# Batch 0's head rearranged: separate PSUM places, no dummy matmuls, other orders on every engine

## The chip, the cores and the metric

The kernel runs on one core of a Trainium2 chip. The metric is the device time of one execution in microseconds (us). Each version is run several times and its median is given; a profiled execution of each version shows what every engine did and when. The engines are TensorE (PE; its weight loads are shown as PEld), VectorE (DVE), ScalarE (ACT), GpSimd (POOL) and SyncE (SP). Each works through its own instruction queue in order, and semaphores tie the queues together. Loads and stores are DMAs, issued from the queues of SP, ACT and POOL.

## The reference

Inputs are q, k and v with 8 batches, 8 heads, 576 positions and 64 columns a head, and the weights of a channel mix: two vectors mu of 512, w_k (512 x 1024), w_v (1024 x 512) and w_r (512 x 512). All are float32.

```
# efficient attention, per batch and head
q_s = exp(q - max) ;  q_s = q_s / sum over d
k_s = exp(k - max) ;  k_s = k_s / sum over s
x   = q_s @ (k_s.T @ v)                 # heads side by side: 8 x 576 x 512
# channel mix, per batch
x_prev = x shifted by one position (first one zero)
xk = mu_k * x + (1 - mu_k) * x_prev ;  xr = mu_r * x + (1 - mu_r) * x_prev
k  = relu(xk @ w_k) ;  v = (k * k) @ w_v ;  r = sigmoid(xr @ w_r)
out = r * v                              # 8 x 576 x 512
```

## The kernel before

**Tiling.** A batch's attention is done in two groups (g = 0, 1) of four heads; a tag such as `01` is batch 0, group 1. A group has two halves (a further digit, 0 or 1), which batches 0 and 1 load and treat one by one. 128 positions-by-head rows lie on the partitions, 9 positions of 64 columns behind each other (`J` = 9). The channel mix works on column units of a ring of four batches (`UNITS`): 11 units in all, each with eight k pieces (`k1_3` is unit 1, piece 3), each followed by `relu` on ScalarE and `sq` (the square) on VectorE. Then come 36 output tiles of 128 positions: `r12` and `v12_0`, `v12_1` are matmuls, `th12` a tanh on ScalarE (the sigmoid), `o12` the gating on VectorE, `st12` the store.

**The steps of batch 0, per group.** `load..` DMAs bring q, k and v. `expq` and `expk` (ScalarE) take exponentials. `rsum` (VectorE) sums each row of q over d, `rrec` takes the reciprocal, `scale` multiplies. `T` (TensorE) turns q, `Z` sums k's exponentials over the positions and `KV` multiplies them with v. `rz` and `kvn` (VectorE) divide the product by those sums. `qt..0` and `qt..1` copy the two halves of the turned q from PSUM, `edge` copies the column that the shift by one needs. `wp` (VectorE or GpSimd) multiplies the small k-v matrix with mu and with 1 - mu: `wp000` for xk (last digit 0) and `wp001` for xr (1). `X` (TensorE) multiplies these with the turned q and its shifted copy, so that attention and the shift's mix are one product: `X0101` is group 01, m = 0 (xk), position half 1. There are eight X groups of eight matmuls in batch 0. Copies in lower case (`x0101a`, `x0010`) take them to the tensors xk and xr, from which the k and r matmuls start. Batch 1 goes the same way (`FUSED`), later batches another way with blocks `TKV` and `B`.

**The mus.** `rows` and `muload` bring the two mu vectors by DMA. `wide` (L273) is a float32 matmul that spreads them over all partitions; `widecopy` (L291) takes it from PSUM, `rest` (L287) computes 1 - mu beside it, and `mucopy` (L296) copies a small turned form. `wp` needs `rest`.

**Dummy matmuls.** `fill` (L303, 19 matmuls of 512 columns) and `fillgap` (L312, 11 of 256 columns) multiply a zeroed tile into PSUM places that nobody reads.

**Orders.** Nothing is scheduled by a compiler. The string `ORDER` lists every step once; each engine gets its steps in that order. A word such as `ACT!qt011:0` gives the engine, the step and the index of the buffer or PSUM place that it takes (`load00v^expq000` waits for expq000 beside its own inputs). GpSimd's queue holds the loads of all batches from 1 on and the weight loads, as well as `wp`s and casts of v.

**PSUM.** There are four single places `mm` and two double places `att`. `any` 0 and 1 are the two `att`, `any` 2 and 3 are pairs of `mm` (`SHARED`). In batch 0 a group's turned q, its sums and its k-v product share one place:

```
qtp = kvp = Slot("any")
```

so that group's place is free only when the q copies and `kvn` have read it.

Of the kernel before, what the change touches and what calls it, by code (L numbers as in the profile page):

```python
# [8 lines left out]
ACT = mybir.ActivationFunctionType  # L9
# [21 lines left out]
         "mm": 4, "att": 2, "any": 4}  # L31
SHARED = {("any", 0): [("att", 0)], ("any", 1): [("att", 1)],
          ("any", 2): [("mm", 0), ("mm", 1)], ("any", 3): [("mm", 2), ("mm", 3)]}
# [13 lines left out]
ident SP!load00q0:0 ACT!load00q1 zero ACT!load01q1:1 SP!load01q0 fill:0 fill.2:1 fill.3:2 fill.4:3  # L47
fill.5:0 fill.6:1 fill.7:2 fill.8:3 fill.9:0 fill.10:1 fill.11:2 fill.12:3 fill.13:0 fill.14:1
# [10 lines left out]
load11k0 k1_0:1 relu1_3:1 sq1_7 k0_5 expq110:2 k0_0:3 load11v0 k1_0.2 k0_0.2 relu0_4:2 rsum110:2  # L59
k1_4:0 relu1_0:0 k1_5:2 sq1_3 expq111 k1_2:1 sq0_4 k1_5.2 sq1_0 k1_2.2 rsum111 relu1_5:1 k1_4.2  # L60
cast111:0 k0_1 relu1_2:2 k0_6:2 sq1_5 wv0 relu1_4:0 k1_6:1 rrec110 expq101:1 sq1_2 k0_2:0
scale110:2 load10k1:9 k0_6.2 relu0_0:1 X0111:1 load10v0 rrec111 k0_7 expq100 rsum101:3 k1_6.2
k1_1:3 relu0_6:2 load10k0 k0_2.2 rrec101 k1_1.2 sq0_0 ACT!x0111 k0_3 rsum100 wv1 r0:2 relu1_1:1
sq0_6 expk111:2 wv2 r1:3 sq1_4 rrec100 th0:0 load20q0:10 scale100:0 relu1_6:2 r2:2 th1:1
load21q0:0 sq1_6 scale111 ACT!cast110 r3:1 sq1_1 relu0_2:0 scale101 T11:0 expk110 T10:1
ACT!cast101:1 KV11 qt101:2 load20v0:1 v3_0:3 qt110:1 sq0_2 th3:2 qt111 v0_0:0 rz11:2 expk101:0
cast100 kvn11:0 DVE!qt100 v1_0:1 edge11 expk100 wp110:0 edge10 DVE!wp111 X1100:0 KV10 x1100 v0_1
rz10:0 kvn10:1 X1111:0 POOL!wp100:1 X1101:1 x1111 v1_1 ACT!x1101 load31q0:2 X1001:0 th2:3 X1000:1
load20k0:3 ACT!x1001 v0_2 DVE!x1000 v3_1 load21v0:4 expq200:0 o0 v1_2 load21k0:5 k2_7:2 k2_3:0
rsum200:1 expq210:2 wp101 k2_7.2 v3_2 load30q0:6 relu2_7:2 o1 X1011:0 X1110:1 cast200:2 load30k0:7  # L70
rrec200 k2_3.2 o3 k2_1:2 load40q0:8 k2_0:1 relu2_3:1 x1011 k2_1.2 load30v0:9 expq310:1 sq2_3
k2_0.2 scale200:1 load41q0:10 k2_2:3 k2_6:0 relu2_1:0 load31k0:0 relu2_0:1 X1010:0 k2_2.2
expk200:1 sq2_0 k2_6.2 DVE!x1010 k2_5:2 load31v0:1 v2_0:1 relu2_2:1 sq2_1 rsum210:0 cast210:0
k2_4:3 load40k0:2 TKV20:0 relu2_6:0 sq2_2 rrec210 expk210:2 k2_4.2 rz20:1 sq2_6 k2_5.2 sq2_7
load40v0:3 v6_0:0 DVE!x1110 relu2_5:1 relu2_4:0 w20:0 v2_1 scale210:2 expq300:0 r5:2 load50q0:4
r6:3 qt20:0 rsum310:2 load50k0:5 v2_2 expk300:0 sq2_5 B21:1.0 sq2_4 o2 load41v0:6 th6:4 v6_1
rz21:2 xb20:0 w21:1 rsum300:3 r4:1 load50v0:7 xs20 qt21:1 r7:3 edge20 o6 th4:5 rrec300 X21:0.1
st6.2 diff20:0 th7:6 r8:0 th5:7 sc2001:0 scale300:0 v4_0:1 xb21:1 v5_0:3 xs21 sc2011:1 cast300:1
sc2010 v7_0:2 sc2000 edge21 rrec310 expq400:2 diff21:1 load70k0:9 TKV30:0 sc2100:2 expq410:0 v5_1
sc2101 load70v0:8 rz30:0 mix210 v4_1 cast310:2 load51v0:10 mix200 v7_1 o5 th8:8 v4_2 load51q0:1  # L80
sc2111:2 k3_1:3 st5.2 expk400:1 o4 w30:2 k3_3:0 st4 o7 relu3_1:2 load41k0:2 st0.2 expk310:2 sc2110
k3_7:1 mix201 st1 k3_0:3 sq3_1 st6 qt30:2 load51k0:0 scale310:1 st5 k3_2:2 relu3_0:1 st1.2
cast400:0 sq3_0 B31:1.0 rsum400:1 relu3_2:0 k3_6:3 load60k0:3 xs30:0 mix211 relu3_7:2 k3_5:2
relu3_3:1 rz31:1 sq3_2 xb30 w31:0 k3_4:1 sq3_3 sq3_7 relu3_6:0 r9:0 edge30 rrec400 diff30:0 qt31:0
r12:3 sq3_6 scale400:2 relu3_5:1 B40:0.1 th9:9 v10_0:2 relu3_4:2 sc3001:0 sq3_5 xs31:1 xb31 sq3_4
r10:0 sc3000 sc3011:1 expk500:0 v10_1 edge31 rsum410:0 v8_0:1 th10:4 load61k0:5 diff31:1 expq500:1
v11_0:0 o10 v8_1 expq510:2 load60v0:4 mix300 r11:2 sc3100:2 th12:7 sc3101 load70q0:1 mix310
cast510:1 v9_0:3 rsum500:3 v11_1 th11:1 load60q0:10 k4_5:2 o8 rz40:2 rrec410 k4_6:1 sc3111:0
relu4_5:0 rrec500 o11 k4_2:2 sc3110 st11.2 sc3010 k5_0:0 scale500:0 st2.2 relu4_2:1 v9_1 st7.2
relu4_6:2 cast410:2 st2 k4_3:2 sq4_2 sq4_5 o9 tq40^load60q0:1 k5_4:1 relu4_3:1 k5_1 scale410:1  # L90
expq600:1 k4_0:3 sq4_6 k5_5 tq41^load60q0:2 relu4_0:0 rsum510:2 k5_6:2 relu5_4:2 k4_1:3 expk410:2
tq50^load60q0:0 w40:1 k4_4:1 sq4_0 sq5_4 relu5_0:0 mix301 k5_7 st11 cast500:0 B41:1.0 mix311 st4.2
relu5_6:2 k4_7:0 st7 rz41:0 sq5_0 rrec510 st0 relu4_1:0 sq4_3 r13:2 rsum600:1 st8 xs40:0 relu4_4:1
# [806 lines left out]
```

## Time and profile before

| what | value |
|---|---|
| median of 3 runs | 196.46 us (196.37 to 196.91) |
| profiled execution | 196.49 us |
| its span, first to last instruction | 194.7 us |
| TensorE busy | 184.9 us (95%) |
| VectorE busy | 148.4 us (76%) |
| ScalarE busy | 133.7 us (69%) |
| GpSimd busy | 46.4 us (24%) |
| DMA | 42.45 MB, 218 GB/s mean |

Rows of the timeline give the start in us from the span's start, the length in us, the engine, the line of the kernel, the operation, the tiles written and read with their shapes, and how many instructions the row holds; a bracket at the end gives the engine's idle time before it and what ended it. In the list of waits, each row gives who waited, for what, the total in us, how often, and the longest. Rows of the chain of waits give start, length and what held up the end of the run. Rows by stretch give, after the stretch and its length, the busy time of TensorE, its weight loads, VectorE, ScalarE and GpSimd (with instruction counts), TensorE's granted clock, the share of the DMA engines that was busy, and GB/s. Matmuls overlap in their pipeline, so the distance between two starts, not a matmul's own length, is its cost in a dense stretch.

### The profile page before, as it was taken

How to read it: one execution, taken by the hardware profiler on the slowest of the kernel's cores; microseconds unless marked ns; L12 is line 12 of the kernel's file. 1: busy time of each engine (PE TensorE's matmuls, PEld its weight loads, DVE VectorE, ACT ScalarE, POOL GpSimd, SP SyncE). 2: the span in 40 equal slices, each digit the busy share in tenths (PEclk: the TensorE clock that was granted, in tenths of full speed). 3: DMA queues.
4: the chain of work that ended last, by engine and by line, in shares of the span. 5: the costliest groups of instructions: out<-in, count | busy, mean ns of one | idle time of the engine just before them, and what ended most of it. 6: DMA issues, size and time to landing. Idle time of an engine off the chain costs nothing.

```text
span 194.7 us, 4639 instructions
## 1 busy us (share of the span) xinstructions
PE 184.9 (95%) x1819; PEld 93.9 (48%) x1841; DVE 148.4 (76%) x343; ACT 133.7 (69%) x214; POOL 46.4 (24%) x76
## 2 busy tenths in 40 slices
PE   7897999999999999999999999999999999999990
PEld 2374755445545544465545644444444444444450
DVE  1886887689999999998998998999669247324431
ACT  3856999899999999489997988663175522621400
POOL 6857663885416303200700000000000000000000
PEclk9999999999999999999999999999999999999998
DMA  5999999999999999979997794144015003703855
GB/s 190 350 204 338 300 306 307 327 397 394 391 392 394 400 411 331 331 246 203 231 407 183 179 206 88 32 100 96 7 35 130 0 0 83 188 3 80 201 123 135
DMA packets 26069, 42.45 MB, mean 218 GB/s; under 512 B 11828, under 2 KB 15168, under 8 KB 26048
## 3 DMA queue, kind: packets, MB, share of 16 engines
q0 software_dynamic: 9504, 28.00, 43.8%
q1 hardware_dynamic: 15728, 12.72, 27.1%
q10 hardware_dynamic: 816, 1.44, 2.0%
q8 instruction: 14, 0.23, 0.5%
q14 instruction: 7, 0.06, 0.1%
HBM read 33.56 MB, written 9.44 MB: 221 GB/s over the span
## 4 chain that ended last, share of the span: by engine, by line
PE 80%; DVE 7%; DMA 6%; issue 2%; ACT 1%; POOL 1%; ACTq 0%; DVEq 0%; POOLq 0%
PE mm_c L681 10%; PE mm_b L734 9%; PE mm_a L734 8%; PE mm_d L734 8%; PE mm_b L681 8%; PE mm_d L681 7%; PE mm_c L714 5%; PE mm_c L734 4%; PE mm_a L681 4%; PE mm_d L714 4%; PE mm_a L714 3%; DMA mu_rows<-in_moe_mu_r_dram 3%; DMA raw_c<-in_q_dram 3%; PE mm_b L714 3%; DVE k L670 1%
## 5 line engine op out<-in xcount | busy, mean ns | idle before, releaser
L734 PEld LDWEIGHTS <-k 128*128 128x128 bf16 x296 | 28.1, 98 | 30.6 <-issue 0.7
L714 PEld LDWEIGHTS <-xr 128*128 128x128 bf16 x144 | 13.9, 98 | 16.4 <-issue 0.2
L670 DVE TENSOR_TENSOR k<-rel_b 128x512 bf16<-128x512 bf16 (+2 forms) x29 | 11.6, 399 | 8.9 <-ACT rel_b L660 8.8
L660 ACT ACTIVATE rel_a<-mm_c 128x512 bf16<-128x512 f32 (+1 forms) x11 | 6.6, 599 | 9.7 <-PE mm_c L681 9.6
L714 PE MATMUL mm_c<-wr,xr 128*128 128x512 bf16 x47 | 12.3, 379 | 0.1
L681 PEld LDWEIGHTS <-wk_aa 128*128 128x128 bf16 x88 | 8.4, 98 | 7.8 <-issue 0.2
L681 PEld LDWEIGHTS <-wk_ba 128*128 128x128 bf16 x88 | 8.3, 98 | 7.8 <-issue 0.4
L670 DVE TENSOR_TENSOR k<-rel_a 128x512 bf16<-128x512 bf16 (+2 forms) x24 | 9.6, 400 | 3.2 <-ACT rel_a L660 3.2
L670 DVE TENSOR_TENSOR k<-rel_c 128x512 bf16<-128x512 bf16 (+2 forms) x23 | 9.3, 403 | 3.4 <-ACT rel_c L660 3.3
L681 PEld LDWEIGHTS <-wk_ab 128*128 128x128 bf16 x88 | 8.4, 98 | 7.1 <-issue 0.5
L681 PEld LDWEIGHTS <-wk_bb 128*128 128x128 bf16 x88 | 8.5, 98 | 6.8
L734 PE MATMUL mm_b<-wv_a,k 128*128 128x512 bf16 x42 | 11.2, 379 | 0.1
L714 PE MATMUL mm_d<-wr,xr 128*128 128x512 bf16 x40 | 10.3, 379 | 0.0
L734 PE MATMUL mm_a<-wv_a,k 128*128 128x512 bf16 x38 | 10.2, 379 | 0.1
L734 PE MATMUL mm_d<-wv_a,k 128*128 128x512 bf16 (+1 forms) x38 | 9.8, 368 | 0.1
L681 PE MATMUL mm_c<-xk,wk_ba 128*128 128x512 bf16 (+3 forms) x34 | 8.6, 334 | 0.0
L681 PE MATMUL mm_c<-xk,wk_bb 128*128 128x512 bf16 (+3 forms) x34 | 8.6, 334 | 0.0
L714 PE MATMUL mm_a<-wr,xr 128*128 128x512 bf16 x31 | 8.2, 380 | 0.1
L660 ACT ACTIVATE rel_c<-mm_c 128x512 bf16<-128x512 f32 (+1 forms) x8 | 4.8, 595 | 4.5 <-PE mm_c L681 2.9
L681 PE MATMUL mm_c<-xk,wk_aa 128*128 128x512 bf16 (+2 forms) x28 | 7.4, 347 | 0.0
L681 PE MATMUL mm_c<-xk,wk_ab 128*128 128x512 bf16 (+2 forms) x26 | 7.0, 344 | 0.0
L660 ACT ACTIVATE rel_b<-mm_d 128x512 bf16<-128x512 f32 (+2 forms) x10 | 5.8, 577 | 1.5 <-PE mm_d L681 1.5
(352 smaller groups left out, 495.4 us busy)
## 6 DMA issues: line engine op xcount, KB each, us to landing
raw_k<-in_q_dram POOLq DMA_DIRECT2D x4, 576.0 KB, 8.1
raw_f<-in_k_dram POOLq DMA_DIRECT2D x3, 576.0 KB, 8.2
raw_a<-in_k_dram POOLq DMA_DIRECT2D x3, 576.0 KB, 11.5
out_dram<-th_b SPq DMA_DIRECT2D x10, 128.0 KB, 2.4
out_dram<-th_c SPq DMA_DIRECT2D x10, 128.0 KB, 2.4
raw_b<-in_v_dram POOLq DMA_DIRECT2D x2, 576.0 KB, 10.4
raw_d<-in_k_dram POOLq DMA_DIRECT2D x2, 576.0 KB, 8.8
raw_e<-in_v_dram POOLq DMA_DIRECT2D x2, 576.0 KB, 6.3
```

What stands on the lines that cost most here:

```text
L660: kn.nc.scalar.activation(out=kn.rels[rel.index][:, 0:width], in_=kn.bank(kf)[:, 0:width], func=ACT.Relu, scale=HALF_ROOT)
L670: kn.nc.vector.tensor_tensor(out=to, in0=src, in1=src, op=ALU.mult)
L681: kn.nc.tensor.matmul(kn.bank(kf)[:, lo:lo + n], lhsT=kn.wk[fc // 4][ct % 2][:, ct // 2, (fc % 4) * 128: (fc % 4) * 128 + 128], rhs=kn.xs[ ...
L714: kn.nc.tensor.matmul(kn.bank(rps), lhsT=kn.xs[1][:, ct, c:c + 128], rhs=kn.wr[:, ct, :], start=(ct == 0), stop=(ct == CT - 1))
L734: kn.nc.tensor.matmul(kn.bank(vps)[:, 0:width], lhsT=kn.k2[:, ft, at:at + 128], rhs=wv_of(ft)[:, part], start=(ft == 0), stop=(ft == FT - 1))
```

## The change

It has five parts.

- In batch 0 the turned q goes to a place of a new kind, `pr` (two pairs of `mm`), and the sums and the k-v product to an `att` place. `KV` now follows `Z` in the same place.
- `rest` (1 - mu) and `mucopy` go from VectorE to ScalarE.
- In batches 0 and 1 reciprocal and scaling of q are done once a group, not once a half. In group 00 and in batch 1 the row sums stay in halves; in group 01 they too become one instruction (`rsum010`).
- The 30 dummy matmuls are left out (`FILLS`, `GAPS`). `WHOLE_Q` is defined and not used.
- `ORDER` is another one from the first step to the last. It also changes the engine of some steps: in batch 1 all four casts of v go to GpSimd (two of them were on ScalarE), in batch 0 `wp010` goes to GpSimd and `wp001` to VectorE (the other way round before), and all eight X groups of batch 0 stand ahead of the first k step (seven before, with `X0111` later).

```
 POOLS = {...
-         "mm": 4, "att": 2, "any": 4}
+         "mm": 4, "att": 2, "any": 4, "pr": 2}
 SHARED = {("any", 0): [("att", 0)], ("any", 1): [("att", 1)],
...
+          ("pr", 0): [("mm", 0), ("mm", 1)], ("pr", 1): [("mm", 2), ("mm", 3)]}
-FILLS = 19
-GAPS = 11
+FILLS = 0
+GAPS = 0
+WHOLE_Q = True
 ORDER = """
-ident SP!load00q0:0 ACT!load00q1 zero ACT!load01q1:1 SP!load01q0 fill:0 fill.2:1 fill.3:2 fill.4:3
...
-fill.15:2 fill.16:3 fill.17:0 fill.18:1 fill.19:2 POOL!rows consts ACT!load00k1:2 SP!load00k0 late
-ACT!load01k1:3 SP!load01k0 warm POOL!muload expq000:0 expq001 load00v^expq000 rsum000:0 rsum001
-load01v expq010:1 wk00 expq011 rrec001 rrec000 rsum010:1 wide:0 wk01 expk000:0 rrec010 rsum011
-wk10 mu:1 expk001 fillgap:2 fillgap.2:3 fillgap.3:2 fillgap.4:3 scale010:0 wk11 Z00:0 fillgap.5:2
-fillgap.6:3 fillgap.7:2 fillgap.8:3 fillgap.9:2 fillgap.10:3 fillgap.11:2 rrec011 expk011:1
-load11q0:4 scale011 widecopy rz00:0 scale001:1 T01:1 KV000 scale000 ACT!qt011:0 KV001 expk010
-DVE!qt010 T00 rest mucopy kvn00:0 KV010 qt001:1 POOL!wp001:0 DVE!qt000 Z01 KV011 edge00 load10q0:5
-wp000 X0010:3 rz01:1 load11q1 X0001:2 kvn01:1 edge01 x0010 wp010:1 load10q1 X0000:0 wp011 x0001a
-X0100:1 load11v1:6 ACT!x0001b X0110:3 x0000a wr X0101:2 x0100b ACT!x0000b x0110 X0011:0 load11k1:7
-DVE!x0101a x0100a k0_4:2 x0101b k1_7:3 x0011 k1_3:0 load10v1:8 k1_7.2 k1_3.2 relu1_7:0 k0_4.2
...
+ident SP!load00q0:0 ACT!load00q1 zero ACT!load01q1:1 SP!load01q0 POOL!rows consts ACT!load00k1:2
+SP!load00k0 late ACT!load01k1:3 SP!load01k0 warm POOL!muload expq000:0 expq001 load00v^expq000
+rsum000:0 rsum001 load01v expq011:1 wk00 expq010 rrec000 scale000:0 wide:0 wk01 expk001:0 wk10
+mu:1 expk000 rsum010:1 T00:1 wk11 Z00:0 expk010:1 load11q0:4 rrec010 rz00:0 scale010:1 widecopy
+load10q1:5 mucopy KV000 load11q1 expk011 KV001 DVE!qt000:0 ACT!qt001 Z01:1 rest kvn00:0 T01:0
+edge00 rz01:1 KV010 wp001:0 ACT!qt011:1 KV011 wp000 X0011:3 kvn01:1 X0000:0 DVE!qt010 POOL!wp010:1
+ACT!x0011 X0010:1 x0000b X0001:2 wr DVE!x0000a x0010 X0101:3 edge01 wp011 ACT!x0001b X0100:0
+load11k0:6 x0001a DVE!x0101a X0110:1 load10q0 ACT!x0101b DVE!x0100a X0111:2 load11k1 k1_3:2
+ACT!x0100b k1_2:3 ACT!x0111 k1_3.2 k1_2.2 relu1_3:0 k1_7:0 load11v1:7 k0_4:1 relu1_2:1 k1_4:2
...
     def emit_rest():
-        kn.nc.vector.tensor_scalar(out=kn.mu_wide[:, 1, :], in0=kn.mu_wide[:, 0, :],
-                                   scalar1=-1.0, scalar2=1.0, op0=ALU.mult, op1=ALU.add)
+        kn.nc.scalar.activation(out=kn.mu_wide[:, 1, :], in_=kn.mu_wide[:, 0, :], func=ACT.Copy,
+                                scale=-1.0, bias=1.0)
...
-    wide_done = add("DVE", emit_rest, [wide_a], name="rest")
+    wide_done = add("ACT", emit_rest, [wide_a], name="rest")
...
+        expq = [add("ACT", lambda u=u: exp(kn.eqs, eq, sq, u), [lq[n], table], [eq], [sq],
+                    name=f"expq{tag}{n}") for n, u in enumerate(us)]
+        if b < 2:
+            parts = us if b or g == 0 else [slice(0, 2)]
+            o = [add("DVE", lambda u=u: rsum(u), expq[u], [stat], name=f"rsum{tag}{n}")
+                 for n, u in enumerate(parts)]
+            o = add("DVE", lambda: rrec(slice(0, 2)), o, name=f"rrec{tag}0")
+            scaled.append(add("DVE", lambda: scale_q(slice(0, 2)), [o], [qs], [eq, stat],
+                              name=f"scale{tag}0"))
...
         if fused:
-            qtp = kvp = Slot("any")
+            qtp, kvp = (Slot("any"), None) if b else (Slot("pr"), Slot("att"))
+            kvp = kvp or qtp
...
-                kvm = [add("PE", lambda u=u: kv(kvp, (u,)), [expk[u], consts, castv[0]], [kvp],
+                kvm = [add("PE", lambda u=u: kv(kvp, (u,)), [zm, expk[u], consts, castv[0]], [],
                            leave_kv, name=f"KV{tag}{u}") for u in range(2)]
```

More of the change, by code (lines that the diff above doesn't have):

```diff
@@ L58 @@
-DVE!x0101a x0100a k0_4:2 x0101b k1_7:3 x0011 k1_3:0 load10v1:8 k1_7.2 k1_3.2 relu1_7:0 k0_4.2
[L59 to L69, printed above, removed]
@@ new lines @@
+relu1_1:2 rz11:2 kvn11:0 ACT!qt101:2 v0_0:1 load21q0:0 qt111:0 DVE!qt110 POOL!wp110:0 expk101:0
+v1_0:2 edge11 qt100 load20v0:1 sq1_1 X1100:0 expk100 v3_0:3 cast100:1 DVE!x1100 th2:3 cast101
+DVE!wp111 X1101:0 load31q0:2 KV10 ACT!x1101 v0_1 rz10:0 load20k0:3 edge10 kvn10:1 X1111:0 wp100:1
+load21k0:4 v1_1 ACT!x1111 sq0_6 X1001:1 load21v0:5 X1000:0 x1001 v0_2 x1000 load30k0:6 v1_2 o0
+expq200:1 k2_7:0 load30q0:7 v3_1 o1 k2_1:1 DVE!wp101 load40q0:8 expq210:2 k2_7.2 rsum200:0 k2_1.2
+X1110:1 relu2_7:1 X1011:0 load41q0:9 cast200:2 k2_3:2 rsum210:1 v3_2 k2_2:0 relu2_1:2 k2_3.2
@@ L311, in fill @@
         def fill(slot=slot):
-            return kn.nc.tensor.matmul(kn.bank(slot)[:, 0:256], lhsT=kn.still[:, 0:128],
-                                       rhs=kn.still[:, 0:256], start=True, stop=True)
+            return kn.nc.tensor.matmul(kn.bank(slot)[:, 0:512], lhsT=kn.still[:, 0:128],
+                                       rhs=kn.still[:, 0:512], start=True, stop=True)
         add("PE", fill, [zero], [slot], [slot], name="fillgap")
@@ L841, in whole @@
     def whole(slot):
-        if slot.pool == "any" and slot.index >= 2:
+        if slot.pool == "pr" or slot.pool == "any" and slot.index >= 2:
             return None
```

133 lines of the change are left out of this document (69 added, 64 removed).

## The prediction

> **What bounds the kernel now.** I read the page first, then TensorE's waits over the whole span, then the head (the first 18 us) row by row. Of the page, the span and the engines:
>
> ```profile
> span 194.7 us, 4639 instructions
> PE 184.9 (95%) x1819; PEld 93.9 (48%) x1841; DVE 148.4 (76%) x343; ACT 133.7 (69%) x214; POOL 46.4 (24%) x76
> ```
>
> A busy TensorE can hide stalls, so the list of its waits decides:
>
> ```profile
> ...
> PE mm_a L273 <- DMA mu_rows<-in_moe_mu_r_dram: 0.9, 1, 0.9
> PE mm_b L521 <- issue: 0.8, 1, 0.8
> PE att_b L420 <- ACT qt_a L396: 0.4, 1, 0.4
> PE att_b L521 <- DVE wp_b L510: 0.2, 1, 0.2
> PE mm_d L734 <- issue: 0.2, 1, 0.2
> PE mm_b L734 <- issue: 0.2, 1, 0.2
> PE mm_a L734 <- DVE th_d L740: 0.2, 1, 0.2
> ```
>
> (The line left out is the wait for the very first fill.) The first four lie before the first k matmul; what follows holds 0.6 us of waiting. From there the kernel is TensorE's own work, which the change leaves as it is. So the time moves with one number: when TensorE reaches unbroken work, and with how much behind it. Before, that is at 17.70, with X0111 (the eighth of batch 0's X groups) still owed:
>
> ```profile
> 17.70 0.39 PE L681 MATMUL mm_c<-xk,wk_ba 128*128 128x256 bf16 x2
> 23.73 0.44 PE L521 MATMUL att_b<-qt_a,wp_b 64*64 64x288 bf16 x8
> 24.10 0.28 PE L681 MATMUL mm_c<-xk,wk_ba 128*128 128x256 bf16 x1
> ```
>
> X0111 takes 24.10 - 23.73 = 0.37 us. The new order has all eight X groups ahead of the first k, so the mark to compare with is 17.70 + 0.37 = 18.07.
>
> **The change, part by part.**
>
> *No fills.* All 30 dummy matmuls go. They stand in TensorE's idle time (nothing real waited for one), so their own time is worth 0. But they also woke the clock:
>
> ```profile
> 1.62 0.63 PE L303 MATMUL mm_b<-rel_c 128*128 128x512 bf16 x1
> 2.05 0.63 PE L303 MATMUL mm_c<-rel_c 128*128 128x512 bf16 x1
> 5.03 0.38 PE L303 MATMUL mm_b<-rel_c 128*128 128x512 bf16 x1
> 5.25 0.38 PE L303 MATMUL mm_c<-rel_c 128*128 128x512 bf16 x1
> 1.22:4.90 3.68, 3.68 (x9) 1.34 (x10) 0.44 (x7) 1.73 (x3) 2.34 (x5) 1.00 0.79 255
> ```
>
> The first fills start 2.05 - 1.62 = 0.43 us apart, from 5.03 on 0.22 apart: half speed for the first 3.8 us after 1.22. (The last row, of the answer by stretches, gives a granted clock of 1.00 there, so that column does not show this state; the spacing does.) Without fills TensorE's first instruction is `wide`, and all of it starts at half speed.
>
> [...]
>
> What then lies behind `wide` on TensorE, in the order before and after, and its durations at full speed:
>
> ```profile
> 2.14 5.97 DMA mu_rows<-in_moe_mu_r_dram
> 8.25 1.09 PE mm_a L273 x2
> 9.82 0.38 PE L407 MATMUL att_a<-one,ek_a 64*128 64x1 bf16 x18
> 11.01 0.44 PE L387 MATMUL att_b<-ident,qs_a 64*128 64x64 bf16 x18
> ```
>
> `wide` waits for a DMA that the change does not touch, so it starts at 8.25 again. At half speed it lasts up to 2 x 1.09 = 2.18, to 10.4; `mu` is small. T00 follows at 10.5: doubled, its 18 transposes keep TensorE 0.5 before Z00 can follow, at 11.0, and Z00 ends after 2 x 0.38, at 11.7. The bounds on the doubling: nothing (Z00 then ends near 10.0), and full; I take full, since the fills are the nearest row.
>
> *Reciprocal and scaling once a group.* These rows price VectorE's queue, which is in order; the first is batch 0, the next are whole-group forms of later batches:
>
> ```profile
> 5.37 1.41 DVE L361 TENSOR_REDUCE rsum_a<-eq_a 128x9 f32<-128x576 bf16 x2 [3.59 <-ACT eq_a L346]
> 38.31 1.35 DVE L361 TENSOR_REDUCE rsum_b<-eq_a 128x18 f32<-128x1152 bf16 x1
> 40.18 0.26 DVE L365 RECIPROCAL rrec_b<-rsum_b 128x18 f32<-128x18 f32 x1
> 41.86 1.35 DVE L370 TENSOR_TENSOR qs_b<-eq_a,rrec_b 128x1152 bf16<-128x1152 bf16 x1
> 10.24 0.17 DVE L427 RECIPROCAL rz_a<-att_a 128x2 f32<-128x2 f32 x1
> 11.66 0.45 DVE L396 COPY qt_a<-att_b 128x576 bf16<-128x576 bf16 x1
> 12.44 0.29 DVE L437 TENSOR_TENSOR kvn_a<-att_a,rz_a 128x128 f32<-128x128 f32 x1
> 13.86 0.20 DVE L504 COPY qt_b<-qt_b 128x126 bf16<-128x126 bf16 x1 [0.76 <-ACT qt_b L396]
> 13.88 0.28 PE L521 MATMUL mm_c<-qt_b,wp_a 64*64 64x288 bf16 x1
> 13.97 0.49 DVE L510 TENSOR_TENSOR wp_a<-kvn_a,mu_wide 128x128 bf16<-128x128 f32 x2
> ```
>
> The new queue, added up: the two row sums of group 0 end at 6.78; rrec000 0.26, scale000 1.35 (8.4); rsum010 1.35, rrec010 0.26 (10.1). Next stands rz00, which needs Z00: VectorE waits from 10.1 to 11.7 with scale010 (1.35) queued behind it. This wait is new; before, Z00 ended at 10.20 behind fills at full speed. Then rz00 0.17 (11.9), scale010 1.35 (13.25), qt000 0.45 (13.7), kvn00 0.29 (14.0), edge00 0.20 (14.2), rz01 0.17 (14.4), wp001 0.49 (14.9). So the first X group starts at about 14.95, against 13.88: 1.1 later.
>
> *1-mu and the small mu copy on ScalarE.* They leave VectorE's queue, where they stood between T00's copy and kvn00. On ScalarE they cost about one `widecopy` (0.57) and a small copy (an estimate of 0.2, from rz00's 0.17):
>
> ```profile
> 9.96 0.57 ACT L291 COPY mu_wide<-mm_a 128x512 f32<-128x512 f32 x1
> 10.43 0.69 ACT L346 ACTIVATE ek_b<-raw_d 128x576 bf16<-128x576 f32 x1
> 12.14 0.64 ACT L396 COPY qt_a<-att_b 128x576 bf16<-128x576 bf16 x1 [1.03 <-DVE qt_a L396]
> ```
>
> ScalarE's queue: widecopy from 10.4 (11.0), mucopy 0.2, expk011 0.69 (11.9), qt001 0.64 (12.55), rest 0.57 (13.1). That is ahead of wp001, which starts at 14.4, so it adds 0; without the late rz00 the cover would be thin (0 to 0.3).
>
> *Places of their own in PSUM.* They remove TensorE's 0.4 us wait for the qt copy (list of waits). Worth 0, because T01 now waits for scale010 (13.25) and KV010 and KV011 end before wp001 does.
>
> *The X phase.* Eight groups at 0.39 each (14.66 - 13.88 = 0.78 for two):
>
> ```profile
> 14.66 0.41 PE L521 MATMUL att_a<-qt_b,wp_a 64*64 64x288 bf16 x8
> 15.81 0.46 DVE L531 CAST xk<-att_b 128x288 bf16<-128x288 f32 x1
> 12.89 0.87 POOL L510 TENSOR_TENSOR wp_a<-kvn_a,mu_wide 128x128 bf16<-128x128 f32 x2 [2.41 <-ACT qt_a L396]
> 36.90 0.76 DVE L533 CAST xk<-att_b 128x576 bf16<-128x576 f32 x1 [0.85 <-PE att_b L521]
> ```
>
> That is 3.1 us of TensorE, but VectorE's queue is longer. After wp001 at 14.9 come wp000 0.49, kvn01 0.29, qt010 0.45, x0000a 0.46, x0010 0.76, edge01 0.20, wp011 0.49: 3.14 together, so wp011 ends at about 18.05. (wp010 goes to GpSimd after kvn01: 15.7 + 0.87 = 16.6, early enough for X0101, and the loads behind it on that queue start that much later, with earlier loads still in flight.) X0110 needs it, X0111 follows, and the first k starts at 18.1 + 2 x 0.41 = 18.95. Against 18.07 that is +0.9; I carry +0.85, since some of the small steps round up. The clock is taken as full by then: TensorE has been busy nearly without a break from 8.25, 6.7 us ahead of the first X.
>
> *The new order behind the head.* TensorE's work there is the same and waits 0.6 us in all, so it can gain at most 0.6; a loss is bounded by the largest single wait in the list, 0.9 once. I take 0. In each group of batch 1 VectorE has one reciprocal and one scaling less to start, and all of that lies beside TensorE: 0. All four casts of batch 1's v go to GpSimd (two were on ScalarE), ahead of loads in its queue; that is a rival below. Both orders end with the halves of v35, their gating and the four last stores: 0.
>
> Sum: 0 (fills' own time) + 0.85 (head) + 0 (rest) + 0 (end). The profiled execution took 196.49, its span 194.7 and 1.8 around it; the median of the runs shown is 196.46, the same to 0.03. **Predicted: 196.46 + 0.85 = 197.3 us.**
>
> **The rivals.**
>
> *A: the half-speed clock costs nothing where it counts (faster).* If `wide`, T00 and Z00 take no longer than now, Z00 ends by 10.0, rz00 waits for nothing, scale010 ends at 11.6, wp001 at 13.3, and the same X queue reaches the first k at 17.3: 0.8 ahead of 18.07, so 195.7. It decides where Z00 ends before 10.8. For it: `wide` uses two rows of the array and Z00 streams one column, so other limits may set their pace. Against it: the fills' spacing, which doubled.
>
> *B: the clock stays at half speed through the X phase (slower still).* TensorE's work from 8.25 to 14.9 is small pieces with gaps, and only the X groups are as dense as the fills were. If the 3.8 us count from 14.95, X groups take 0.8 until 18.7 (4.7 of them), then 3.3 x 0.41: the first k comes at 20.05, 1.1 later than in the sum, at 198.4.
>
> [...]
>
> *C: a new wait behind the head.* The casts are the likeliest place:
>
> ```profile
> 30.87 0.92 POOL L353 CAST vv_b<-raw_i 128x576 bf16<-128x576 f32 x1 [0.53 <-DMA raw_i<-in_v_dram]
> 33.78 0.48 PE L420 MATMUL att_b<-vv_b,ek_a 64*64 64x65 bf16 x36
> ```
>
> In the new order both halves of v of group 10 land last, where now the last half of v (cast from 30.87 on, when it had landed) and one of k come, and are cast one behind the other, 0.92 each. Landing by an estimated 31.5, they are ready at 33.4, and KV10 comes at 33.78 + 0.85: 1.2 us of room. If the landing slips by over 1.2, TensorE stops; I price one wait of 0.9, so 198.2.
>
> **How the numbers follow.** The sum holds with 0.50 (its own range 196.8 to 197.8: half or all of the doubling, some wait more or less); A 0.17; B 0.17; C 0.16. About 0.3% (0.6 us) is what a measurement can tell from no change. A is faster; of the main case a third comes in under 197.05 (a doubling that is not full, and up to 0.6 of waits gone), which with a mild A makes 0.2 the same; B, C and the rest are slower: 0.17, 0.20, 0.63. The range runs from A's 195.7 to just over B's 198.4, with C on top of the sum inside: 195.7 to 198.8.
>
> **What would show it.** Right: `wide` takes about 2 us, Z00 ends at 11.5 to 11.8, rz00 is what ends VectorE's longest wait in the head, X starts near 14.9 and the first k near 18.9, and TensorE's waits behind it stay under 1 us. Rival A shows as a `wide` of 1.1 us; B as X groups 0.8 apart; C as a TensorE wait on a cast, or on anything else, behind 20 us. The prediction fails if `wide` or the X phase has another pace than computed, or if the new order brings waits behind the head that the old one hasn't.

## The result and the profile after

The changed kernel takes 196.14 us (median of 20 runs, 195.28 to 196.95); the kernel before, on the same chip, 196.66 (20 runs, 196.37 to 197.13). The ratio is 0.9969, with a 95% interval of 0.9958 to 0.9981: 0.5 us, or 0.3%, faster. Predicted were 197.3 us, and slower with a chance of 0.63. The runs of after spread over 1.67 us, those of before over 0.76. Its profiled execution is its fastest (195.28), so a second profile, of the same kernel run again (`e3_after_again`, 196.61), is read beside it.

The page of after, its span and engines, and then its whole list of TensorE's waits:

```profile
span 193.5 us, 4601 instructions
...
PE 180.7 (93%) x1811; PEld 92.6 (48%) x1811; DVE 150.8 (78%) x335; ACT 132.6 (69%) x213; POOL 47.8 (25%) x76
```

```profile
PE mm_a L271 <- DVE qs_a L368: 8.3, 1, 8.3
PE att_a L418 <- DVE rz_a L425: 0.3, 1, 0.3
```

The first of the waits is the start, up to `wide` (L271); here the list puts it down to VectorE, in the second profile to the load of the mus. Of the waits that before had, the `issue: 0.8` and the 0.4 for the q copy are gone. The head of after, by its timeline (start, length, engine, line, tiles, count, and in brackets the idle time ahead of it):

```profile
8.26 2.04 PE L271 MATMUL mm_a<-mu_rows,pick 2*128 2x512 f32 x2 [8.26 <-DVE qs_a L368]
...
10.71 0.41 PE L405 MATMUL att_a<-one,ek_a 64*128 64x1 bf16 x18
...
11.16 0.17 DVE L425 RECIPROCAL rz_a<-att_a 128x2 f32<-128x2 f32 x1 [1.34 <-PE att_a L405]
11.25 1.34 DVE L368 TENSOR_TENSOR qs_b<-eq_b,rrec_b 128x1152 bf16<-128x1152 bf16 x1
...
12.50 0.45 DVE L394 COPY qt_a<-mm_d 128x576 bf16<-128x576 bf16 x1
...
12.87 0.28 DVE L435 TENSOR_TENSOR kvn_a<-att_a,rz_a 128x128 f32<-128x128 f32 x1
...
13.25 0.47 DVE L518 TENSOR_TENSOR wp_a<-kvn_a,mu_wide 128x128 bf16<-128x128 f32 x2
...
13.98 0.45 PE L529 MATMUL mm_c<-qt_a,wp_a 64*64 64x288 bf16 x1
...
14.46 0.64 PE L529 MATMUL att_a<-qt_a,wp_a 64*64 64x288 bf16 x8
...
14.84 0.50 PE L529 MATMUL att_b<-qt_a,wp_a 64*64 64x288 bf16 x8
...
15.47 0.66 ACT L541 CAST xr<-att_b 128x576 bf16<-128x576 f32 x1
...
15.97 0.48 DVE L518 TENSOR_TENSOR wp_b<-kvn_b,mu_wide 128x128 bf16<-128x128 f32 x2
...
17.16 0.44 PE L689 MATMUL mm_c<-xk,wk_aa 128*128 128x320 bf16 x2
```

`wide` is doubled, 2.04 against 1.09, as the prediction says, and `rz00` does end a wait of VectorE, 1.34. But the first X group comes at 13.98 instead of 14.95 and the first k at 17.16 instead of 18.95. The X groups start 13.98, 14.46, 14.84: half speed for two of them, then full.

The end, in the timeline of before and then of after (ACTq and SPq are the issues of stores from ScalarE's and SyncE's queues):

```profile
188.72 0.55 ACTq L750 DMA_DIRECT2D out_dram<-th_d  x1
...
189.39 0.60 ACT L719 ACTIVATE th_b<-mm_a 128x512 f32<-128x512 f32 x1 [5.06 <-PE mm_d L734]
...
189.76 0.38 PE L734 MATMUL mm_c<-wv_c,k 128*128 128x256 bf16 x2
190.02 0.42 DVE L740 SCALAR_TENSOR_TENSOR th_b<-th_b,mm_d 128x256 f32<-128x256 f32 x1 [1.33 <-ACT th_b L719]
190.36 0.41 DVE L740 SCALAR_TENSOR_TENSOR th_b<-th_b,mm_c 128x256 f32<-128x256 f32 x1
```

```profile
188.10 0.60 ACT L727 ACTIVATE th_a<-mm_c 128x512 f32<-128x512 f32 x1 [1.13 <-PE mm_c L722]
...
188.16 0.55 ACTq L758 DMA_DIRECT2D out_dram<-th_h  x1
...
188.73 0.42 DVE L748 SCALAR_TENSOR_TENSOR th_a<-th_a,mm_a 128x256 f32<-128x256 f32 x1 [0.75 <-ACT th_a L727]
...
188.99 0.38 PE L742 MATMUL mm_d<-wv_c,k 128*128 128x256 bf16 x2
...
189.41 0.42 DVE L748 SCALAR_TENSOR_TENSOR th_a<-th_a,mm_d 128x256 f32<-128x256 f32 x1 [0.26 <-PE mm_d L742]
```

Before, ScalarE's queue issues a store of tile 34 (0.55) and only then runs the last tanh, at 189.39; the gating waits for that tanh (1.33) and its second half starts 0.6 after the last matmul row does. After, the tanh stands ahead of that issue and has long been done, and the last gating waits for TensorE alone. The stretch from the start of TensorE's last matmul (189.87 and 189.10) to the end of the span falls from 4.79 to 4.41.

So the profiled executions (194.7 and 193.5 of span) differ by: head -0.91 (17.16 against the mark of 18.07), from there to the last matmul +0.14 (189.10 - 17.16 = 171.94, against 189.87 - 18.07 = 171.80), end -0.38; together -1.15 of the 1.2. The second profile of the same kernel (`e3_after_again`), by its timeline:

```profile
14.45 0.87 PE L529 MATMUL att_a<-qt_a,wp_a 64*64 64x288 bf16 x8
...
14.93 0.87 PE L529 MATMUL att_b<-qt_a,wp_a 64*64 64x288 bf16 x8
...
16.85 0.87 PE L529 MATMUL att_b<-qt_b,wp_b 64*64 64x288 bf16 x8
...
17.97 0.45 PE L689 MATMUL mm_c<-xk,wk_aa 128*128 128x320 bf16 x2
```

All X groups run at half speed here (0.87 a group's row against 0.50, 0.48 between starts), and the first k comes at 17.97: head -0.10. The dense part is 172.45 (+0.65), the end -0.38 again: together +0.17, where the spans differ by +0.1. The 0.5 us of the medians lie between these two: the end's 0.4 in both, the head's gain and what follows it in some. Of the 1.3 us between the two executions, 0.8 lie ahead of the first k and 0.5 behind it.

### The profile page after: what moved, and what is told of

The parts are those of the page before. It is cut to its first block, busy times and chain, and to the rows that moved or that the text cites. A ratio compares the mean times of both kernels' runs of the same rounds, so it can differ in the third digit from the quotient of the medians.

```text
span 193.5 us, 4601 instructions
## 1 busy us (share of the span) xinstructions
PE 180.7 (93%) x1811; PEld 92.6 (48%) x1811; DVE 150.8 (78%) x335; ACT 132.6 (69%) x213; POOL 47.8 (25%) x76
## 3 DMA queue, kind: packets, MB, share of 16 engines
q10 hardware_dynamic: 816, 1.44, 2.1%
## 4 chain that ended last, share of the span: by engine, by line
PE 92%; DVE 2%; DMA 2%; issue 1%; ACT 0%
PE mm_b L689 10%; PE mm_d L742 9%; PE mm_b L742 9%; PE mm_c L742 9%; PE mm_a L689 9%; PE mm_d L689 7%; PE mm_c L689 7%; PE mm_c L722 6%; PE mm_a L742 5%; PE mm_a L722 4%; PE mm_d L722 3%; PE mm_b L722 3%; DMA raw_a<-in_q_dram 2%; PE att_b L418 2%; PE att_a L529 1%; PE att_b L585 1%
## 5 line engine op out<-in xcount | busy, mean ns | idle before, releaser
L678 DVE TENSOR_TENSOR k<-rel_c 128x512 bf16<-128x512 bf16 (+2 forms) x29 | 12.0, 413 | 8.4 <-ACT rel_c L668 8.2
L678 DVE TENSOR_TENSOR k<-rel_b 128x512 bf16<-128x512 bf16 (+2 forms) x24 | 9.8, 409 | 5.4 <-ACT rel_b L668 5.4
L742 PE MATMUL mm_c<-wv_a,k 128*128 128x512 bf16 x40 | 10.3, 380 | 0.0
L668 ACT ACTIVATE rel_c<-mm_b 128x512 bf16<-128x512 f32 (+1 forms) x7 | 4.3, 616 | 8.6 <-PE mm_b L689 8.6
L271 PE MATMUL mm_a<-mu_rows,pick 2*128 2x512 f32 x2 | 2.0, 1122 | 8.3 <-DVE qs_a L368 8.3
L689 PE MATMUL mm_b<-xk,wk_ba 128*128 128x512 bf16 (+2 forms) x32 | 8.2, 338 | 0.0
L689 PE MATMUL mm_b<-xk,wk_bb 128*128 128x512 bf16 (+2 forms) x32 | 8.2, 337 | 0.0
L590 ACT CAST xb_a<-att_b 128x1024 bf16<-128x1024 f32 x6 | 6.1, 1024 | 2.9 <-DVE xr L612 1.5
L722 PE MATMUL mm_d<-wr,xr 128*128 128x512 bf16 x28 | 7.2, 380 | 0.0
L722 PE MATMUL mm_b<-wr,xr 128*128 128x512 bf16 x28 | 7.2, 379 | 0.0
## 6 DMA issues: line engine op xcount, KB each, us to landing
raw_d<-in_k_dram POOLq DMA_DIRECT2D x3, 576.0 KB, 11.7
```

The costliest lines, as they stand in the source:

```text
L271: kn.nc.tensor.matmul(kn.bank(wide_slot), lhsT=kn.pick[:].rearrange("p u c -> p (u c)"), rhs=kn.mu_rows[:].rearrange("p m c -> p (m c)"), ...
L590: kn.nc.scalar.copy(out=kn.xbs[xb.index][:, :, 64:576], in_=kn.whole(pair))
L668: kn.nc.scalar.activation(out=kn.rels[rel.index][:, 0:width], in_=kn.bank(kf)[:, 0:width], func=ACT.Relu, scale=HALF_ROOT)
L678: kn.nc.vector.tensor_tensor(out=to, in0=src, in1=src, op=ALU.mult)
L689: kn.nc.tensor.matmul(kn.bank(kf)[:, lo:lo + n], lhsT=kn.wk[fc // 4][ct % 2][:, ct // 2, (fc % 4) * 128: (fc % 4) * 128 + 128], rhs=kn.xs[ ...
L722: kn.nc.tensor.matmul(kn.bank(rps), lhsT=kn.xs[1][:, ct, c:c + 128], rhs=kn.wr[:, ct, :], start=(ct == 0), stop=(ct == CT - 1))
```

## The experiments

The first question was which part brings the gain. My theories: the end (a tanh ahead of a store's issue), and the dummies, in two ways: they warm the clock, and, as a guess, 30 matmuls more bring TensorE sooner to instructions that have not landed yet. The rival to the second: only the clock counts.

**The end alone.** Before with `th35` moved up, first past v35_0 only (another engine), then past ScalarE's store too; and after with before's end:

```
 e4:  ... st34.2 st34 th35:1 v35_0:2 st33.2 v35_1        (th35 behind st34.2 still)
 e8:  ... st34 th35:1 v35_0:2 st34.2 st33.2 v35_1
 e9:  after, ... st34.2 st34 v35_0:3 th35:0 o35.2 v35_1
```

> The kernel before with the last tanh (th35) listed ahead of the matmuls v35_0 and not behind them. These are on different engines, so on ScalarE the tanh still stands behind the issue of a store of tile 34 (0.55 us from 188.72). If that issue is what holds the tanh until 189.39, nothing moves: 196.6. If it is the wait for the matmuls, the tanh starts at 188.9 and the end comes 0.2 us earlier.

> The kernel before with one thing of the changed kernel's end: the last tanh (th35) stands on ScalarE ahead of the issue of tile 34's second store, not behind it. If that issue (0.55 us from 188.72) holds the tanh, it now starts at 188.9 in place of 189.39, the two last gatings end 0.2 us earlier and so does the run: 196.45 against 196.7. If the end is not set there: 196.7.

> The changed kernel with the end's order of before: tile 34's second store is issued on ScalarE ahead of the last tanh. Theory (the end is worth 0.4 us, the larger part of the whole gain): the tanh comes 0.5 us later, the last TensorE instruction to the end takes 4.8 in place of 4.4 us, 196.5 against 196.1 to 196.4. If the gain is in the head alone: no change.

Measured: e4 196.67 (0.9986, 0.9971 to 1.0001), no change that can be told; e8 196.37 (0.9981, 0.997 to 0.9993), 0.37 us faster; e9 196.49 (0.9988, 0.9966 to 1.0009), 0.35 slower than after's 196.14. In e8's timeline the tanh comes ahead of the issue:

```profile
188.72 0.60 ACT L719 ACTIVATE th_b<-mm_a 128x512 f32<-128x512 f32 x1 [4.53 <-PE mm_a L714]
...
188.78 0.54 ACTq L750 DMA_DIRECT2D out_dram<-th_d  x1
...
189.35 0.42 DVE L740 SCALAR_TENSOR_TENSOR th_b<-th_b,mm_d 128x256 f32<-128x256 f32 x1 [0.80 <-ACT th_b L719]
...
190.03 0.42 DVE L740 SCALAR_TENSOR_TENSOR th_b<-th_b,mm_c 128x256 f32<-128x256 f32 x1 [0.26 <-PE mm_c L734]
```

e9's stretch from the last matmul's start to the end is 4.92, against after's 4.41. Both directions agree with the two profiles' 0.38: one store's issue ahead of one tanh. By the medians that is most of the 0.5; e8's interval is clear of 1, while e9's overlaps after's, so there the trace carries the point.

**The dummies.** Before without its 30; before with them one column wide (as many instructions, hardly any work); before with five long float32 ones (work, few instructions); after with 19 of the old ones; after with five and with three long ones:

```
 e2:  FILLS = 0, GAPS = 0                      e1 (after): FILLS = 19, GAPS = 0
 e5:  matmul(kn.bank(slot)[:, 0:1], lhsT=kn.still[:, 0:128], rhs=kn.still[:, 0:1])
 e6:  FILLS = 4, GAPS = 1, kn.still = kn.ths[-1]   (float32)
 e7 (after): the same, slots in "att", fillgap:1 behind Z00     e10 (after): FILLS = 3
```

> The changed kernel with the 19 dummy matmuls of before put back at the start, nothing else. Theory 1 (the half-speed clock costs the changed kernel 0.5 to 1.5 us, and how much differs from run to run with the moment at which full speed comes): wide about 1.1 us in place of 2.04, the first X group ahead of 13.98, the first k at 16.4 to 16.9, a median of 194.6 to 195.3 and a spread of at most that of the kernel before (0.8 us), where the changed kernel has 1.7. Theory 2 (the clock does not count, the spread comes from the DMAs): 196.1 and the spread as it is.

> The kernel before without any of its 30 dummy matmuls, its order otherwise kept. Theory 1: wide takes 2.0 us and Z00 and the rest of the chain come later, the first k 0.8 to 1.5 us after 17.70, 197.5 to 198.2, with a spread of over 1.2 us. Theory 2: 196.6 and a spread of 0.8.

> The kernel before with all 30 dummy matmuls kept but each one column wide: as many TensorE instructions as before, no warming. New theory (code): the dummies cost 0.8 to 1.1 us because they push TensorE's 450th instruction into the X phase, ahead of the landing of a 16 KB block of its code, and they save about as much by the full clock, so that leaving them out of the kernel before changed nothing (196.67). Then this one has both costs: wide 2.0 us, X groups at half speed and a stop after 449 instructions, 197.1 to 197.8. Old theory (clock alone, no cost of the dummies): 196.7 as without them.

> The kernel before with five long float32 dummy matmuls of 512 columns (four at the start, one behind Z00) in place of the 30 short ones. Code theory: warm and without the stop, so wide 1.1 us, no wait of 0.8 in the middle of an X group, the first k near 16.9, 195.6 to 196.1. If float32 dummies do not wake the clock: wide 2.0 us or later by a fill, 196.7 to 197.7. Old theory: 196.7.

> The changed kernel with the same five long float32 dummies (the fifth into a free att place, behind Z00, where TensorE waits for v). Code theory: wide 1.1 us, X from 12.8 at full speed, no stop at instruction 450, the first k near 16.2, 194.2 to 194.8, and a spread of under 1 us. If only the clock counts and not the stop: 195.3, as with the 19 short ones.

> The changed kernel with three long float32 dummies at the start and none later. The 449th TensorE instruction then comes after 9 k matmuls, near 17.0, where the code has landed by then. Code theory: wide 1.1 us, X from 12.5 at full speed, the first k near 15.7 and no stop of over 0.5 us behind it, 194.2 to 195.0. If the stop does not count: as with five, 195.4. If the clock falls back in the idle time between the third dummy (6.4) and wide, X groups run at half speed and it is 195.3 to 196.3.

> The changed kernel once more, for the second profile. The first profile is of its fastest run (195.28, median 196.14). Theory 1: in a profile of a slower run the X groups stay at half speed for longer (in the first one they reach full speed near 14.9), the first k comes as much later than 17.16 as the run is slower than 195.28, and the stretch from the first k to the end is the same. Theory 2: the X groups run alike and the time is lost behind the first k.

| kernel | median us | ratio to before, 95% | `wide` | first X | first k |
|---|---|---|---|---|---|
| before | 196.66 | 1 | 1.09 | 13.88 | 17.70 |
| after | 196.14 | 0.9969 (0.9958 to 0.9981) | 2.04 | 13.98 | 17.16 |
| e3, after again | 196.43 | 0.9968 (0.9951 to 0.9985) | 2.04 | 13.97 | 17.97 |
| e1, after + 19 dummies | 195.29 | 0.993 (0.9906 to 0.9953) | 1.09 | 12.75 | 17.60 |
| e2, before without | 196.67 | 1.0017 (0.9992 to 1.0041) | 2.04 | 14.47 | 17.71 |
| e5, one column wide | 197.31 | 1.0032 (1.0015 to 1.0048) | 2.04 | 14.36 | 18.07 |
| e6, before, five long | 196.78 | 1.0005 (0.9989 to 1.002) | 1.09 | 13.73 | 17.16 |
| e7, after, five long | 195.41 | 0.9941 (0.9925 to 0.9958) | 1.09 | 12.51 | 15.68 |
| e10, after, three long | 195.43 | 0.9935 (0.9916 to 0.9954) | 1.09 | 12.89 | 16.19 |

The last three columns are of one profiled execution each, in which `wide` starts between 7.80 and 8.45; e1's took 196.38, 1.1 above its median. The kernel before, e2, e5 and e6 still owe one X group behind the first k.

Three things follow. First, the clock is real: with work in the dummies `wide` takes 1.09, without it 2.04, in every row of the table. Second, the dummies can bring on a stop, which the prediction put at 0. In e7 TensorE stops, and the list names nothing that it waits for; the waits, the timeline, and the queues on its page:

```profile
PE mm_c L691 <- issue: 1.2, 1, 1.2
```

```profile
15.68 0.31 PE L691 MATMUL mm_c<-xk,wk_aa 128*128 128x320 bf16 x1
17.19 0.30 PE L691 MATMUL mm_c<-xk,wk_aa 128*128 128x320 bf16 x1 [1.20 <-issue]
```

```profile
q8 instruction: 14, 0.23, 0.5%
```

The stop comes behind the same count of recorded TensorE instructions, 222 matmuls and 222 or 223 weight loads, in before (16.12 to 17.20), e1 (16.05 to 17.23, put down there to a copy on ScalarE, which ended at 15.86), e7 (15.69 to 17.19) and e10 (16.75 to 17.17), and in e4, e8, e15 and e16, though the instruction there is another in the two orders and with other dummies. 14 packets of instructions came over the DMA engines, of about 16 KB each by the page's total (0.23 MB); the first of the run starts at 14.9 in e7. In the eight profiles with a stop this first packet starts at 14.64 to 15.11, and the stop ends 2.2 to 2.4 later, at 16.99 to 17.40, however early it began. Kernels that reach that count later do not stop: e5 at about 17, and so e13 (of the last question below); after, e2 and e3 behind 18. What TensorE saves ahead of the stop is waited out: e7's first k is at 15.68 and its second matmul at 17.19, the time of after's first k. That the stop is the wait for such a packet is my reading of the count and the times, not something the trace states.

Third, the two do not add as I expected. e5 was built to have the stop without the work, and its time came out as expected, but its list of TensorE's waits has no stop:

```profile
PE mm_a L273 <- DVE rrec_b L365: 6.0, 1, 6.0
PE mm_a L303 <- DVE qt_c L250: 1.2, 1, 1.2
PE att_b L420 <- ACT qt_a L396: 0.2, 1, 0.2
```

All its X groups run at half speed, and it comes to the count at 17.0, where the next instruction follows at 17.20. So the time fits for another reason: without work in its dummies, the kernel before is 0.6 slower (197.31), with no stop to blame. e2, which has neither, missed the clock theory's 197.5 to 198.2 by its median, 196.67; its runs reach up to 198.73. e6, which has the work and no stop, missed its expectation of 195.6 to 196.1 with 196.78. Its first k waits 0.4 for a copy and stands at 17.16, 0.54 ahead of before's; its profiled span is 0.4 shorter than before's (194.3), but 2.3 us lie around that span instead of 1.8, and what else held the median is open. So the traces show the stop, and no median shows what it costs the kernel before.

e1 met its time (194.6 to 195.3), not its first k (16.4 to 16.9) nor its spread (0.8; it is 1.44). e7 and e10 missed theirs (194.2 to 194.8 and 194.2 to 195.0): in e7 the stop takes the head's lead back; in e10 it is short, and TensorE waits 0.5 twice behind the head, once for a cast of batch 1's v. Even so e1, e7 and e10 beat both kernels, by 1.4, 1.3 and 1.2 us against before: leaving the dummies out was a loss for after, 0.85 by e1.

**The parts in batch 0.** Each taken back alone, from after:

```
 e11:  rest and mucopy on VectorE again (nc.vector.tensor_scalar, tensor_copy)
 e12:  qtp = kvp = Slot("any") in batch 0;  T00:0 wk11 Z00 ... Z01:1 rest kvn00:0 T01
 e14:  rsum, rrec and scale of batch 0 by halves (batch 1 as after)
```

> The changed kernel with 1-mu and the small mu copy back on VectorE, at the same places of the order. VectorE's queue from rz00 to wp001 then holds 0.4 + 0.16 us more, and wp001 sets the first X group: the first X near 14.5 in place of 13.98. Theory (VectorE's queue sets the head): 0.3 to 0.6 slower than the changed kernel, 196.5 to 196.9. If the head is hidden by something else (weights that land, the code): 196.1 to 196.4.

> The changed kernel with turned q, sums and k-v product of a group in one shared att place, as before. rz and the q copies then wait for more than they need: the first X group comes 0.1 to 0.6 later than 13.98, and the run 196.2 to 196.9. If the separate places bring nothing in this order: 196.1 to 196.4 and the first X near 13.98.

> The kernel after with the reciprocal, the scaling and group 01's row sums of batch 0 done once a half again; batch 1 stays as it is after. If the merged forms shorten VectorE's chain to the first X group, that chain grows by three or four short instructions of 0.1 to 0.2 us each: first X 0.2 to 0.5 later, 196.4 to 196.8 us. If the chain ahead of the X phase has room (as the prediction priced the merge, by its long instructions alone), 196.1 to 196.3 as after.

e12 takes 198.28 (1.007, 1.0046 to 1.0095), 2.1 above after. Its TensorE waits:

```profile
PE att_b L418 <- DVE rz_b L425: 0.7, 1, 0.7
PE att_b L418 <- DVE qt_b L394: 0.5, 1, 0.5
PE att_a L418 <- DVE rz_a L425: 0.3, 1, 0.3
```

The product of group 01 waits for the q copy (0.5), as it must with one place; its first X comes at 15.09 and its first k at 19.07. e11 takes 196.93 (1.0006, 0.9985 to 1.0028), 0.8 above after; its first X is 0.26 later than after's, all its X groups run at half speed in the profile, and the first k is at 18.40. e14 takes 195.90 (0.9955, 0.9931 to 0.9979), 0.2 below after, where 196.4 to 196.8 was what a worthwhile merge would have given: in batch 0 the merged reciprocal and scaling bring nothing. These prices are each for one part undone in an order made for all of them; they do not add up to the 0.5. The new order by itself, without the other parts, was not run.

**Why no version gets far below 195.3.** e7's first k is 1.5 ahead of after's and its last matmul only 0.04. Beside the stop, batch 1's v was a suspect: it is cast at the same 26.1 and 27.4 us in after, e7 and e10. e13 is e10 without the loads of w_v (w_v is zero, so its output lacks the second product of the channel mix), e15 is e7 with two casts ahead of two w_v issues, e16 is e15 with one later load's issue ahead of the next two casts:

```
 e13:  wv0 wv1 wv2 on VectorE: memset(kn.wv[i][:], 0.0)
 e15:  ... cast111:0 ... cast110 wv1 wv2 th1:1        (before: wv1 ... cast111 ... wv2 ... cast110)
 e16:  ... v3_0:3 load31q0:2 cast100:1 ... cast101 ... (load31q0 behind the casts in e15)
```

> The kernel after with three long dummies, with w_v not loaded: its three tiles are set to zero by VectorE instead, so the second product of the channel mix is left out of what it computes, while every matmul is still issued. This takes 2 MB and three issues out of GpSimd's queue ahead of batch 1's casts of v. The floor theory (supply): no version came below about 195.2 us because batch 1's v is cast at fixed times (26.1 and 27.4 us of the span) whatever the head gained, so KV11 and what follows stop for it; with the queue free the casts come earlier, the waits of about 0.5 us at KV11 go, and the time falls from 195.43 to 194.6 to 195.1. Rival (the floor is not there, the head's lead is lost in TensorE's own pace): 195.3 to 195.5, with the casts earlier and nothing gained.

> The kernel after with five long dummies, with the two casts of batch 1 group 1's v moved ahead of two issues of w_v loads in GpSimd's queue. If these issues hold the casts, the casts start up to 0.7 us earlier, KV11 no longer waits, and the time falls from 195.41 to 194.9 to 195.2. If the casts wait for the landing of v itself, their start stays at about 26.1 and 27.4, and the time stays at 195.3 to 195.5 or rises a little, since w_v lands later.

> The kernel of the run with the casts first, with one issue of a later load (0.73 us of GpSimd's queue) put ahead of group 10's two casts of v, so that they start about 0.7 us later, at 32.5 of the span. In that run VectorE's edge copy lasted 1.57 us where it takes 0.17 elsewhere: it started at 31.58 and ended as GpSimd's casts (31.81 to 33.10) did, and TensorE waited 1.23 us for it. If the casts hold VectorE (lock theory), the edge copy falls to under 0.5 us, TensorE's wait of 1.23 goes, and at most 0.5 comes back where KV10 waits for the later casts: 195.2 to 195.9. If the copy is long for another reason (rival), it stays at 1.3 us or more and the time at 196.3 to 196.7.

e13 takes 195.51 (0.9943, 0.9915 to 0.9972), no better than e10: the supply theory falls in the form that I gave it. GpSimd's timeline of e13:

```profile
25.84 2.40 POOL L353 CAST vv_a<-raw_h 128x576 bf16<-128x576 f32 x2 [1.49 <-DMA raw_h<-in_v_dram]
```

With 2 MB taken out the first cast still waits for v to land, at 25.84. In this profile TensorE has neither e10's wait for the cast nor its stop, and the execution is e13's fastest (194.92, under e10's 195.21); the median did not follow, and more can't be said with a spread of 2.4 us.

e15 was to be faster, or as fast to a little slower, and takes 196.47 (0.9981, 0.996 to 1.0002), 1.06 more than e7. The casts did not hold KV11 there; two others stood beside a long copy on VectorE. e15's timeline, VectorE, GpSimd and TensorE:

```profile
31.58 1.57 DVE L514 COPY qt_a<-qt_a 128x126 bf16<-128x126 bf16 x1 [0.76 <-ACT qt_a L396]
...
31.81 1.29 POOL L353 CAST vv_b<-raw_j 128x576 bf16<-128x576 f32 x2
...
33.21 0.32 PE L531 MATMUL att_a<-qt_a,wp_a 64*64 64x288 bf16 x4 [1.23 <-DVE qt_a L514]
```

The edge copy takes 0.17 elsewhere; here 1.57, and it ends (33.15) as the casts do (33.10). In e16 the casts start at 32.34:

```profile
31.39 0.56 DVE L514 COPY qt_a<-qt_a 128x126 bf16<-128x126 bf16 x1 [0.76 <-ACT qt_a L396]
...
32.34 1.28 POOL L353 CAST vv_b<-raw_j 128x576 bf16<-128x576 f32 x2
...
32.00 0.32 PE L531 MATMUL att_a<-qt_a,wp_a 64*64 64x288 bf16 x4 [0.22 <-DVE qt_a L514]
```

The copy falls to 0.56 (under 0.5 was expected), TensorE's wait from 1.23 to 0.22, and the median to 195.67 (0.9973, 0.9946 to 0.9999), inside the 195.2 to 195.9 that was given if the casts hold VectorE. e16's runs fall in two groups, 195.42 to 195.69 (seven) and 196.96 to 197.09 (five); that the second is the same collision is a guess that no trace here shows. What keeps the medians of e1, e7, e10 and e13 at 195.3 to 195.5 stays open.

The same collision stands in after. VectorE and GpSimd in its profile, and then in `e3_after_again`:

```profile
31.53 0.39 DVE L512 COPY qt_a<-qt_a 128x126 bf16<-128x126 bf16 x1 [0.76 <-ACT qt_a L394]
31.82 0.31 DVE L678 TENSOR_TENSOR k<-rel_c 128x320 bf16<-128x320 bf16 x1
...
31.92 1.35 POOL L351 CAST vv_b<-raw_j 128x576 bf16<-128x576 f32 x2
```

```profile
32.77 0.92 DVE L678 TENSOR_TENSOR k<-rel_c 128x320 bf16<-128x320 bf16 x1
...
32.81 1.39 POOL L351 CAST vv_b<-raw_j 128x576 bf16<-128x576 f32 x2
...
33.74 0.82 PE L742 MATMUL mm_d<-wv_a,k 128*128 128x512 bf16 x3 [0.20 <-DVE k L678]
```

Where the head is late, the square of k (0.31) runs into the casts, takes 0.92, and TensorE waits for it (0.20); where it is early, copy and square start ahead of them and keep 0.39 and 0.31. That is part of the +0.65 in the second profile.

## Why the prediction was wrong

Two terms of the sum failed: the head's +0.85, and the 0 for the end. The time lies inside the stated range, at the end where rival A stood, but not by A's mechanism, so that is luck.

- *No fills, own time 0*: not shown. TensorE's `issue` wait of 0.8 stands in the prediction's list, which gave it no cause: it is the stop behind a fixed count of instructions, and the dummies brought TensorE to it sooner. Without them it is gone (e2), and the warmth is too; e2's median is before's, so there the two about cancel.
- *Half speed of `wide`*: right, 2.04 where up to 2.18 was said. *Of T00*: right too; from its start at 10.24 to Z00's at 10.71 it takes 0.47, where 0.5 was said. *Of Z00*: wrong. Z00's row is 0.41 against 0.38 before, not 0.76, and it ends at 11.12 instead of 11.7: 18 matmuls of one column took 0.03 more where `wide` took 0.95 more.
- *The VectorE chain to the first X*: mis-summed. The prediction added durations (3.2 from rz00 to the end of wp001). The rows overlap: 11.16 to 13.72 is 2.56 (scale010 starts 0.09 after rz00, which is a 0.17 row). With Z00 0.58 early, wp001 ends at 13.72 instead of 14.9; the first X starts 0.26 behind it, at 13.98, 0.97 ahead of the forecast.
- *The X phase*: wrong. VectorE's queue of 3.14 ahead of wp011 held x0010 (0.76), which is ScalarE's (15.47, in the rows above), and again whole durations; it left out x0000b, which is VectorE's (two casts from 15.14, 0.82). wp011 ended at 16.45, not 18.05, and the eight X groups, not VectorE, set the first k. *The clock is full by then*: wrong in part, since X groups ran at half speed, for two groups or for all eight. So head +0.85 became -0.91 in one profile and -0.10 in the other.
- *PSUM places, 0, and 1-mu on ScalarE, 0*: wrong in this order; undone alone they cost 2.1 and 0.8. *The merged reciprocal and scaling*: no gain in the run for batch 0, and none in the sum.
- *The order behind the head, 0*: right in the first profile (+0.14), not in the second (+0.65).
- *The end, 0*: wrong, and it is the largest sure part. "Both orders end with the halves of v35" compared TensorE's steps and left out the one that had moved on ScalarE: tanh and store changed places, -0.37.

Rival A had the sign, but failed by its own signs: `wide` took 2.04 and not 1.1, and Z00 ended at 11.12, not before 10.8. It was right of Z00's own length alone. e1 is the run that gives A its condition (`wide` 1.09, Z00 from 9.54 on): 195.29 where A said 195.7. So the half-speed clock, priced at 1.6 between A and the sum, cost after 0.85. Rival B came true for the X phase, at 0.48 a group and not 0.8; the first k came 0.8 us later in the second profile than in the first, not 1.1. The X groups start at half speed behind 3.7 us (10.24 to 13.98) of transposes and matmuls of up to 64 columns; no run here separates the kind of that work from its lightness. Rival C had the place, the casts, and the wrong way: what cost time was not that their results were late but that a copy on VectorE ran long beside them (1.57 in e15, with TensorE waiting 1.23).

## What to carry to other kernels

Read every wait of the bound engine that the profile calls `issue`: if it stands behind the same count of instructions in another version, it may be a price on instructions. Dummies that warm the clock can then take back what they give: e7's first k came 1.5 ahead of after's, and its second matmul at 17.19, against 17.16 for after's first. That a few long ones are better than many short ones is not shown here (195.41 with five, 195.29 with 19). When an order is new, compare every queue at the very end, not the bound engine's alone; one store's issue ahead of the last activation cost 0.4 us. Sum a chain by the distances between starts (2.56 here), not by the lengths of rows (3.2), and take each step's engine from the code.

## What had not been expected of the hardware

- A stop of TensorE behind 444 or 445 recorded instructions that ends, in eight profiles, at 17.0 to 17.4 us, 2.2 to 2.4 after the first packet of instructions starts, whenever the stop began (15.7 to 16.75).
- The clock fell back. In e10 the column of the granted clock shows it, with 1.00 for 8.30 to 9.50, 0.88 for 9.50 to 11.00, and then (stretch, length, busy PE, PEld, DVE, ACT, POOL, granted clock, DMA share, GB/s):

```profile
11.00:12.80 1.80, 1.73 (x76) 1.55 (x72) 1.80 (x8) 1.80 (x4) 0.38 (x1) 0.50 1.23 203
12.80:14.30 1.50, 1.50 (x53) 1.46 (x47) 0.89 (x5) 0.62 (x3) 0.51 (x2) 0.59 1.25 206
```

This is behind three long dummies and a `wide` of 1.09; between `wide` and the X groups TensorE had only matmuls of up to 64 columns, and that their lightness let the clock go is my reading. e1, with its 19 dummies, has 0.50 from 12.80 to 16.00; e7, with a fifth long dummy behind Z00, has 9 tenths or more in every slice of its page. In `e3_after_again`, where it had not yet been up, the same column says 1.00 while X groups run at 0.48 instead of 0.35 to 0.39: here the column does not show the half-speed time. The moment of full speed lies near 14.7 in one profile of after and past 17.3 in another.
- VectorE ran long beside GpSimd's casts: 1.57 for a copy of 0.17 (e15), 0.92 for a product of 0.31 (`e3_after_again`). In e15 the copy ends 0.05 behind the casts, as if they held it. But there the copy's row starts 0.23 ahead of the cast, while GpSimd issues a load until 31.8, and which of them held what the trace does not show; e16's copy takes 0.56 beside issues of loads alone.
